# The forward recurrence pinned to one written order, with column-tiled matmuls in a few long blocks and the fold of the chain in fp32

## The chip, the cores and the metric

The kernel runs on one core of a Trainium2 chip. Its time is the device time of one execution, from the first to the last instruction with a little around it; the median of several executions is quoted. The engines have names as in the profile: PE is TensorE (PEld its weight loads), DVE is VectorE, ACT is ScalarE, POOL is GpSimd, and SP is SyncE, which here only issues DMA transfers.

## The reference

Forward and backward pass of one transformer block with conditioning. The part around the change is the attention, which is a recurrence: 2048 rows are cut into 64 segments of 32 rows, and each segment attends over 8 memory rows and its own 32 rows, where the memory is the first 8 output rows of the segment before.

```python
for s in range(n_seg):                                  # 64 segments
    h = concatenate([mem, x[:, s*32:(s+1)*32]], axis=1) # 8 + 32 rows, 512 wide
    q, k, v = h @ Wq, h @ Wk, h @ Wv                    # 32 heads of 128
    p = softmax(where(mask, q @ k.T * scale, -1e9))
    o = (p @ v) @ Wo                                    # 40 rows, 512 wide
    mem = o[:, :8]                                      # to the next segment
    outs.append(o[:, 8:])
```

Around it stand a layer norm with scale and shift, a gated MLP with its own layer norm, and the gradients of all inputs and weights.

## The kernel before

The program has five stages: the forward recurrence (`phase2`, with the first layer norm, `phase1_setup`, worked in between), the MLP forward and backward (`phase3`), weight gradients of the MLP, the backward recurrence (`phase4`) and the weight gradients of the attention (`phase5`). The change touches `phase2` and helpers that it calls.

`phase2` loops over segments `s`; `s4 = s % 4` is the place in a group of four segments, that is of 128 rows. In one segment:

- `hT` holds 8 memory columns and 24 columns of the layer-normed input, transposed. `proj(x, hf, eng)` multiplies it by one half of the heads of Wq, Wk or Wv: 16 column-tiled matmuls (stationary operand 32 columns wide, four of them side by side in the array, each to its own 32 partitions of a PSUM bank `pass_ps`), and `eng` copies the bank to rows `RA..`. `turn(x, hf, eng)` transposes these rows with four full-array matmuls (`turn_ps`) and `to_heads` spreads them over `QT`, `KT` or `VT` with three copies on `eng`.
- The last 8 rows of the four segments of a group don't depend on the chain. Their projections (`proj_b`, from `hb`, 16 column-tiled matmuls each) and transposes (`turn_b`) are put as pieces in named slots of the segments (`b_pieces`, `fill`); `to_heads("pool", ...)` copies them in.
- `st_exp(pi)` makes scores of four (the last time three) groups of heads and ACT writes their exponentials to `ET`. `vst(pi)` transposes V, `den(pi)` sums the denominators and DVE inverts them (`rden`), `pv(pi)` multiplies by V and DVE scales into `Ost`, `ott(pi)` transposes to `OT`.
- `outproj` multiplies `OT` by `Wo`: 32 column-tiled matmuls that add up in four column groups of one bank, `at_ps`. The four groups must be added: `fold_split` makes a bf16 high part (ACT, `at_hi`) and a bf16 rest (DVE, `at_lo`) of each half of the bank, and `fold_sum` adds the groups with eight small matmuls against `foldsel` (`at_ft`). ACT copies 8 columns of `at_ft` into the next segment's `hT`. That closes the chain. `TailRows` does the same for the last 8 rows of each group (`ao_tps`), in pieces called by `tail.chunk()`.
- A transposing DMA turns `ET` into `Pst`; POOL multiplies it by `rden` (`norm`), and SP stores it (`PS`). Other stores go through SP too: rows of K and Q (`KST`, `QST`), `VT`, `Ost` (`OSR`), `OT`.
- `p1(j, k)` is step `k` of the layer norm of 128 rows two groups ahead: 0 loads the rows, 1 takes their statistics (`BN_STATS` on DVE), 2 scales them, 3 shifts them, stores them and transposes them.

A scheduler turns the program into one instruction order for each engine: it takes the instructions by its own estimate of when they could start, so what stands in an engine's queue need not be the order of the code. Each engine then works its queue strictly in order and waits at an instruction whose semaphores are not there yet. SP works its DMA issues in order in the same way.

Of the kernel before, what the change touches and what calls it, by code (L numbers as in the profile page):

```python
# [40 lines left out]
class K:  # L41
# [73 lines left out]
    def phase0(self):  # L115
# [10 lines left out]
        nc.vector.tensor_tensor(self.foldsel[:], fs2[:, 0, :], fs2[:, 1, :], op=ALU.add)  # L126
        self.later = []
# [117 lines left out]

    def fold_split(self, pool, ps, name):
# [3 lines left out]
        for h in range(2):  # L250
            sl = slice(256 * h, 256 * h + 256)
            hi = pool.tile([128, 256], BF16, name=name + "_hi", tag=f"hi{h}")
            nc.scalar.activation(hi[:], ps[:, sl], AF.Copy)  # L253
            parts.append(hi)
        for h in range(2):
            lo = pool.tile([128, 256], BF16, name=name + "_lo", tag=f"lo{h}")
# [52 lines left out]
    def phase1_setup(self, ctx, psum_tile_fn):  # L309
# [11 lines left out]
        def p1_tile(j):  # L321
# [23 lines left out]
            def turn():  # L345
                h1 = p1w.tile([128, D], BF16, name="h1", bufs=1)
                nc.vector.tensor_tensor(h1[:], st["xh"][:], sa_bc[:], op=ALU.add)
                nc.gpsimd.dma_start(self.H1ROWS[j * 128:(j + 1) * 128, :], h1[:])
                tp = psum_tile_fn()
                for c in range(DC):  # L350
                    nc.tensor.transpose(tp[:, c, :], h1[:, c * 128:(c + 1) * 128], self.ident[:])
# [6 lines left out]
            return load, stats, scale, turn  # L358
# [11 lines left out]
    def phase2(self):  # L370
# [6 lines left out]
        with ExitStack() as ctx:  # L377
# [45 lines left out]
            def p1(j, k=None):  # L423
                if j < NT:
                    if j not in p1s:
                        p1s[j] = p1_tile(j)
                    for i in (range(1, 4) if k is None else [k]):
# [6 lines left out]
            with tc.tile_pool(name="p0", bufs=1) as p0:  # L434
# [10 lines left out]
                p1(0, 3)  # L445
                for f in zeros:
# [72 lines left out]
            def b_pieces(t):  # L519
# [17 lines left out]
                return {(0, "end1"): [P("v", 0)], (1, "end1"): [P("v", 1)], (1, "end2"): [P("k", 0)], (2, "mid"): [T_("v")],  # L537
                        (2, "end1"): [P("k", 1)], (2, "end2"): [P("q", 0)], (3, "end1"): [P("q", 1)], (3, "end2"): [T_("k")],
                        (4, "start"): [T_("q")]}

            first = b_pieces(0)
            q_first = [first.pop(k)[0] for k in ((2, "end2"), (3, "end1"), (4, "start"))]
# [11 lines left out]
            tail = TailRows(self, sb2, psp, psb, 1, "ao", self.AOB)  # L554
            for s in range(NS):
                s4 = s % nseg_t
                if s4 == 0:
                    p1(s // nseg_t + P1_AHEAD, 0)
                    carried = slots.pop((4, "start"), [])
                    slots = {}  # L560
                    if s + nseg_t < NS:
                        slots.update(b_pieces(s // nseg_t + 1))
# [5 lines left out]
                bt = btails[s // nseg_t]  # L568
# [6 lines left out]
                def turn(x, hf, eng):  # L575
                    if hf == 0:
                        to_heads("pool", XT[x], bt[x][:], 0, 8, 32, 8, 8 * s4)
# [1128 lines left out]
```

## Time and profile before

| | |
|---|---|
| median of three runs | 3587.64 us (3587.45 to 3591.0) |
| the profiled execution | 3587.19 us, of which the span of the instructions is 3585.4 us |
| PE | 3262.0 us busy, 39586 matmuls |
| DVE / ACT / POOL | 1655.4 / 1189.8 / 1077.9 us busy |
| mean granted TensorE clock | 0.966 of full |
| the recurrence, 60 to 1285 us | PE busy 1097 of 1225 us, granted clock 0.96, DMA engines busy 0.64 |

A busy PE is no PE at its peak: matmuls overlap, so that busy times of a group say less than the distance from the start of one to the start of the next. The time of the recurrence is best read as the distance from one segment's copy into `hT` to the next one's.

### The profile page before, as it was taken

What the parts mean: (1) busy time and instruction counts of PE and PEld (TensorE: products, weight loads), DVE (VectorE), ACT (ScalarE), POOL (GpSimd) and SP (SyncE); (2) the same over time, 40 slices, a digit from 0 to 9 for tenths busy, and PEclk for the clock granted to TensorE, in tenths of its full rate; (3) what the DMA queues carried; (4) which work ended last, traced back from release to release, by engine and by line L of the source; (5) the groups of instructions that cost most, each with busy time, mean ns of one, the idle gap of its engine ahead of it and who ended that gap; (6) DMA issues with size and microseconds to landing.
All of it is one profiled execution on the core that took longest, in us unless ns stands there. A gap on an engine that the chain in (4) does not pass through costs nothing.

```text
span 3585.4 us, 96873 instructions
## 1 busy us (share of the span) xinstructions
PE 3262.0 (91%) x39586; PEld 1763.8 (49%) x39662; DVE 1655.4 (46%) x4224; ACT 1189.8 (33%) x2714; POOL 1077.9 (30%) x2260
## 2 busy tenths in 40 slices
PE   5898899888899968996998999999999996999999
PEld 2555455455555534442554555555555553445454
DVE  4444444445454447674234555555555552322212
ACT  2444444444454433332122333333333331100011
POOL 2333333333333325553112222222222221322321
PEclk8999999999999989998999999999999998999999
DMA  8566656566676668886789999999999998887776
GB/s 272 125 135 138 139 131 134 128 134 129 132 137 142 146 177 212 202 199 188 230 230 213 236 240 240 230 242 237 236 241 239 239 228 218 232 217 200 205 199 171
DMA packets 880890, 692.19 MB, mean 193 GB/s; under 512 B 591014, under 2 KB 756150, under 8 KB 880316
## 3 DMA queue, kind: packets, MB, share of 16 engines
q1 hardware_dynamic: 786204, 501.90, 63.0%
q0 software_dynamic: 39488, 135.58, 11.9%
q10 hardware_dynamic: 54752, 48.50, 5.1%
q8 instruction: 311, 5.10, 0.6%
q14 instruction: 135, 1.11, 0.1%
HBM read 292.29 MB, written 275.02 MB: 158 GB/s over the span
## 4 chain that ended last, share of the span: by engine, by line
PE 41%; issue 6%; DMA 3%; POOL 2%; ACT 0%; DVE 0%; SPq 0%; POOLq 0%; ACTq 0%; DVEq 0%
PE dh_ps L211 10%; PE gps L1514 7%; PE pass_ps L222 5%; PE g_ps L1257 4%; PE dh_tps L211 3%; PE gps5o L1524 3%; PE gps L994 3%; PE tps L1189 2%; DMA rows<-OSR 1%; PE dp_ps L1243 1%; PE turn_ps L229 1%; PE dp_ps L1247 1%; POOL out_dram L1518 1%; DMA Kst<-KST 1%; PE dh_ft L266 1%
## 5 line engine op out<-in xcount | busy, mean ns | idle before, releaser
L1514 PE MATMUL gps<-rows,hrows 128*128 128x512 bf16 (+2 forms) x2124 | 415.1, 355 | 1.9
L1514 PEld LDWEIGHTS <-hrows 128*128 128x128 bf16 x2160 | 211.3, 98 | 204.0
L711 POOL TENSOR_TENSOR Pst<-Pst,rden 120x1408 bf16<-120x1408 bf16 x64 | 162.1, 2532 | 429.8 <-DMA Pst<-ET 295.8
L222 PEld LDWEIGHTS <-hT 128*32 128x32 bf16 x6144 | 166.8, 99 | 141.9 <-issue 24.0
L63 DVE CAST ot<-gps 128x512 bf16<-128x512 f32 (+3 forms) x77 | 48.8, 634 | 372.0 <-PE gps L1514 201.9
L257 DVE TENSOR_TENSOR dh_lo<-dh_ps,dh_hi 128x256 bf16<-128x256 f32 x128 | 48.3, 419 | 330.5 <-ACT dh_hi L253 330.5
L211 PE MATMUL at_ps<-Wo,OT 128*32 128x512 bf16 x2048 | 174.6, 384 | 22.3 <-ACT OT L61 22.3
L61 ACT ACTIVATE dVT<-g_ps 128x512 bf16<-128x512 f32 (+1 forms) x192 | 107.8, 561 | 249.9 <-issue 107.9
L61 ACT ACTIVATE ot<-gps 128x512 bf16<-128x512 f32 (+3 forms) x77 | 42.4, 550 | 397.1 <-PE gps L1514 251.9
L1518 POOL DMA_DIRECT2D out_dram<-ot x108 | 81.2, 752 | 284.9 <-DVE ot L63 142.2
L222 PE MATMUL pass_ps<-Wv,hT 128*32 128x512 bf16 x2048 | 144.3, 425 | 5.2 <-ACT hT L700 5.2
L61 ACT ACTIVATE OT<-tps 128x512 bf16<-128x512 bf16 (+1 forms) x192 | 107.7, 561 | 121.8 <-PE tps L608 92.9
L211 PE MATMUL dh_ps<-WvT,dVT 128*32 128x512 bf16 x2048 | 145.8, 383 | 0.0
L61 ACT ACTIVATE dQT<-g_ps 128x512 bf16<-128x512 f32 (+1 forms) x192 | 107.8, 561 | 109.9 <-PE g_ps L1257 107.1
L1524 PE MATMUL gps5o<-dyrows,rows 128*128 128x512 bf16 x588 | 134.9, 388 | 3.9 <-DMA rows<-OSR 3.3
L222 PE MATMUL pass_ps<-Wk,hT 128*32 128x512 bf16 x2048 | 137.4, 384 | 0.0
L211 PE MATMUL dh_ps<-WkT,dKT 128*32 128x512 bf16 x2048 | 134.0, 382 | 0.0
L222 PE MATMUL pass_ps<-Wq,hT 128*32 128x512 bf16 x2048 | 134.0, 382 | 0.0
L622 DVE TENSOR_TENSOR Ost<-or_ps,rden 120x512 bf16<-120x512 f32 (+1 forms) x192 | 124.0, 646 | 15.8
L257 DVE TENSOR_TENSOR at_lo<-at_ps,at_hi 128x256 bf16<-128x256 f32 x128 | 48.2, 418 | 173.9 <-PE pass_ps L222 151.1
L222 PE MATMUL pass_ps<-WoT,dyT 128*32 128x512 bf16 x2048 | 123.5, 383 | 4.9 <-ACT dyT L1330 4.9
L63 DVE CAST dKT<-g_ps 128x512 bf16<-128x512 f32 (+1 forms) x192 | 122.3, 637 | 10.9 <-PE g_ps L1257 9.5
(379 smaller groups left out, 7275.6 us busy)
## 6 DMA issues: line engine op xcount, KB each, us to landing
OSR<-Ost SPq DMA_DIRECT2D x64, 352.0 KB
OT<-OT SPq DMA_DIRECT2D x64, 352.0 KB
PS<-Pst SPq DMA_DIRECT2D x64, 352.0 KB
OT_l<-OT SPq DMA_DIRECT2D x64, 352.0 KB
Pst_l<-PS SPq DMA_DIRECT2D x64, 352.0 KB
DVR<-rows_x POOLq DMA_DIRECT2D x64, 352.0 KB, 4.7
DKR<-rows_x POOLq DMA_DIRECT2D x64, 352.0 KB, 5.7
DQR<-rows_x POOLq DMA_DIRECT2D x64, 352.0 KB, 4.2
```

Of the source, the lines that this page charges most:

```text
L61: return nc.scalar.activation(out, in_, AF.Copy)
L63: return nc.vector.tensor_copy(out, in_)
L211: self.nc.tensor.matmul(ps[32 * j:32 * j + 32, :], lhsT=lhsT, rhs=w, start=(n < 4), stop=(n >= total - 4), tile_position=(0, 32 * j))
L222: self.nc.tensor.matmul(ps[32 * j:32 * j + 32, :], lhsT=lhs(c), rhs=rhs, start=(c == 0), stop=(c == DC - 1), tile_position=(0, 32 * j))
L257: nc.vector.tensor_tensor(lo[:], ps[:, 256 * h:256 * h + 256], parts[h][:], op=ALU.subtract)
L622: nc.vector.tensor_tensor(part3(Ost, pi)[0:120, 0:n, :], or_ps[0:120, 0:n, :], rden[:, pi * PG:pi * PG + n].unsqueeze(2).to_broadcast([120 ...
L711: nc.gpsimd.tensor_tensor(Pst[0:120, :, :], Pst[0:120, :, :], rden[:, :].unsqueeze(2).to_broadcast([120, G, 128]), op=ALU.mult)
L994: nc.tensor.matmul(ps[:], lhsT=h2r[:, j, c * 128:(c + 1) * 128], rhs=xr[:, j, :], start=(j == 0), stop=(j == NT - 1))
L1257: nc.tensor.matmul(ps[:, j, :], lhsT=lh[:, g * GW:(g + 1) * GW], rhs=rh[:, g * GW:(g + 1) * GW], start=True, stop=True)
L1514: nc.tensor.matmul(ps[:, 0:ng * E], lhsT=hrows[:, tp_, c * 128:(c + 1) * 128], rhs=rows[:, tp_, 0:ng * E], start=(tp_ == 0), stop=(tp_ == ...
L1518: nc.gpsimd.dma_start(outw[c * 128:(c + 1) * 128, h0:h0 + 3 * (ng - 1) + 1:3, :], ot[:, 0:ng * E].rearrange("p (h e) -> p h e", e=E))
L1524: nc.tensor.matmul(ps[:], lhsT=rows[:, tp_, gg * E:(gg + 1) * E], rhs=dyrows[:, tp_, :], start=(tp_ == 0), stop=(tp_ == NTP - 1))
```

## The change

- Order: `pin` ties every instruction that the loop over segments issues to the one before it on its engine, in the order of the code. The scheduler can no longer move any of them past another, on PE, DVE, ACT, POOL or SP.
- The code of a segment is written in a new order: six `proj` in a row, then six `turn`, one piece of 16 column-tiled matmuls (slot `f1`) behind the first scores, a second one (slot `f2`) behind `outproj`, which now is one block of 32. The tail's chunks are two of 16, both in the fourth segment.
- The fold: ACT copies the left half and DVE the right half of `at_ps` as fp32 to one tile `at_part`, and four fp32 matmuls against an fp32 `foldsel32` replace eight bf16 ones.
- Engines: `turn` of K and Q goes to DVE and of V to ACT; the last copy to `OT` goes to DVE.
- Layer norm: step 0 is at the start of a group as it was, the statistics now stand in the second segment behind the projections of V; shift and transposes are two steps.
- `Pst`'s transposing DMA is issued right behind the last scores, `Ost` and `OT` are stored before the fold instead of at the end, `norm` moves to the start of the next segment, and the copies of the group's last rows (`tails_in`) are made one segment ahead.

```diff
+    def pin(self, i0):
+        last = {}
+        for ins in self.traced()[i0:]:
+            e = ins.engine
+            if e in last:
+                self.tc.add_manual_dep(ins, last[e].name, ..., reason="program order")
+            last[e] = ins
+    def fold_parts(self, pool, ps, name):
+        t = pool.tile([128, 512], F32, name=name + "_part", tag="part", bufs=1)
+        self.evac("act", t[:, 0:256], ps[:, 0:256])
+        self.evac("dve", t[:, 256:512], ps[:, 256:512])
+        return t
+    def fold32(self, psp, part, name, tag):
+        ft = psp.tile([128, self.cfg.DC, 32], F32, name=name + "_ft", tag=tag)
+        for c in range(self.cfg.DC):
+            self.nc.tensor.matmul(ft[:, c, :], lhsT=part[:, c * 128:(c + 1) * 128], rhs=self.foldsel32[:], start=True, stop=True)
+        return ft
...
+                return {(0, "f1"): [P("v", 0)], (0, "f2"): [P("v", 1)], (1, "f1"): [P("k", 0)], (1, "f2"): [P("k", 1)], (1, "w4"): [T_("v")],
+                        (2, "f1"): [P("q", 0)], (2, "f2"): [P("q", 1)], (2, "w4"): [T_("k")], (3, "turn"): [T_("q")]}
...
+                if norms:
+                    norms.pop()()
                 proj("v", 0, "act")
                 proj("v", 1, "dve")
-                if s4 == 0:
-                    for f in carried:
-                        f()
+                if 1 <= s4 <= 3:
+                    p1(s // nseg_t + P1_AHEAD, s4)
                 proj("k", 0, "act")
-                turn("v", 0, "dve")
+                proj("k", 1, "dve")
+                proj("q", 0, "dve")
+                proj("q", 1, "act")
...
-                proj("q", 0, "dve")
+                turn("k", 0, "dve")
+                turn("q", 0, "dve")
+                turn("v", 0, "act")
                 turn("v", 1, "act")
+                turn("k", 1, "dve")
+                turn("q", 1, "dve")
                 nc.sync.dma_start(self.VT[s], VT[:, :])
...
                 st_exp(0)
                 vst(0)
+                fill(s4, "f1")
+                if s4 == 3:
+                    tail.chunk()
+                st_exp(1)
                 vst(1)
-                self.pop_later()
                 vst(2)
                 den(0)
                 pv(0)
-                st_exp(1)
                 st_exp(2)
-                fill(s4, "mid")
+                fill(s4, "turn")
...
+                    tails_in("kqv", s + 1)
+                Pst = sb2.tile([128, G, 128], BF16, name="Pst", bufs=1)
+                nc.sync.dma_start(Pst[:], ET[:, :], transpose=True)
...
                 ott(2)
-                if norms:
-                    norms.pop()()
-                outproj(12, 24)
-                outproj(24, H)
-                parts = self.fold_split(sb2, at_ps[0], "at")
+                nc.sync.dma_start(self.OSR[s], gl3(Ost))
+                outproj(0, H)
+                part = self.fold_parts(sb2, at_ps[0], "at")
                 tail.collect(s4, [OT])
-                fill(s4, "end1")
+                nc.sync.dma_start(self.OT[s], gl3(OT))
+                fill(s4, "f2")
...
-                ft = self.fold_sum(psp, parts, "at", "p")
+                ft = self.fold32(psp, part, "at", "p")
...
+            self.pin(i0)
```

Three places of the resulting order matter for what follows. First DVE, in the queue between the last scaling into `Ost` and the fold. Before, at the end of a group's fourth segment, the statistics of a layer-norm tile (`x_1` is the tile of loaded rows) stand ahead of the bf16 rest of the fold:

```order
L622 TENSOR_TENSOR Ost_157<-or_ps,rden 120x384 [waits DVE_49]
L331 BN_STATS st_13901<-x_1_13274 128x6 [waits DMAHW0_49]
L333 BN_AGGR mv_13903<-st_13901 128x2 [waits DVE_49]
L335 TENSOR_SCALAR ve_13905<-mv_13903 128x1 [waits DVE_49]
L257 TENSOR_TENSOR at_lo<-at_ps,at_hi 128x256 [waits PE_49,Activation_49]
```

Now, from the end of a group's first segment into the second, the same engine has:

```order
L653 TENSOR_TENSOR Ost_159<-or_ps,rden 120x384 [waits DVE_49,PE_49]
L63 COPY OT_160<-tps 128x384 [waits DMAHW5_49,PE_49,Pool_49]
L63 COPY at_part<-at_ps 128x256 [waits Activation_49]
L63 CAST RBv_166<-pass_ps 128x512 [waits PE_49]
L302 CAST at_tb<-at_ft 128x128 [waits Activation_49]
L63 CAST RA0v_161<-pass_ps 128x512 [waits PE_49]
L359 BN_STATS st_11884<-x_1_11467 128x6 [waits DMAHW6_49]
L361 BN_AGGR mv_11886<-st_11884 128x2 [waits DVE_49]
L363 TENSOR_SCALAR ve_11888<-mv_11886 128x1 [waits DVE_49]
L63 CAST RA1k_164<-pass_ps 128x512 [waits DMAHW7_49,PE_49]
```

The statistics moved from the end of the fourth segment to the second segment, behind the fold; the right half of the fold waits for ACT, whose half of the same bank comes first.

On PE at the fold in a group's second segment, before:

```order
L222 LDWEIGHTS hb
L222 MATMUL pass_ps<-Wv,hb 32x512
L266 LDWEIGHTS at_hi
L266 MATMUL at_ft<-foldsel,at_hi 128x32
L222 LDWEIGHTS hb
L222 MATMUL pass_ps<-Wk,hb 32x512
```

and now:

```order
L224 LDWEIGHTS hb
L224 MATMUL pass_ps<-Wk,hb 32x512
L271 MATMUL at_ft<-foldsel_94,at_part 128x32 x4
L231 LDWEIGHTS RBv_166
L231 MATMUL turn_ps<-ident,RBv_166 128x128
```

Full-array matmuls of the fold no longer stand between column-tiled ones; `x4` are the four fp32 matmuls, which have no weight-load instruction of their own in this list.

On SP, from the transposing DMA of a group's fourth segment to that of the next segment, before:

```order
L683 DMA_TRANSPOSE Pst<-ET_155 128x11x128
L327 DMA x_1_19602<-in_A_x_dram 128x512
L707 DMA OSR<-Ost_157 128x1408
L708 DMA OT<-OT_158 128x1408
L713 DMA PS<-Pst 128x1408
L510 DMA QST<-RBq_166 4x8x1024 x3
L513 DMA QST<-RBq_166 4x8x384 x2
L652 DMA VT<-vT_154 128x1328
L504 DMA KST<-RA0k_160 3x32x1024
L506 DMA KST<-RA0k_160 32x3x384
L504 DMA QST<-RA0q_161 3x32x1024
L506 DMA QST<-RA0q_161 32x3x384
```

and now:

```order
L710 DMA_TRANSPOSE Pst<-ET_157 128x11x128
L725 DMA OSR<-Ost_159 128x1408
L729 DMA OT<-OT_160 128x1408
L355 DMA x_1_13013<-in_A_x_dram 128x512
L744 DMA PS<-Pst 128x1408
L535 DMA KST<-RA0k_162 3x32x1024
L537 DMA KST<-RA0k_162 32x3x384
L535 DMA QST<-RA0q_163 3x32x1024
L537 DMA QST<-RA0q_163 32x3x384
L691 DMA VT<-vT_156 128x1328
L710 DMA_TRANSPOSE Pst<-ET_157 128x11x128
```

The store of `Pst` now has only stores of rows and of `VT` between itself and the next transposing DMA; the stores of the group's last rows (`RBq`) no longer stand there.

More of the change, by code (lines that the diff above doesn't have):

```diff
@@ L356, in turn @@
                 return hx, hb
-            return load, stats, scale, turn
+            return load, stats, scale, shift, turn
         return p1_tile
@@ L426, in p1 @@
                         p1s[j] = p1_tile(j)
-                    for i in (range(1, 4) if k is None else [k]):
+                    for i in (range(1, 5) if k is None else [k]):
                         r = p1s[j][i]()
@@ L445, in phase2 @@
                 p1(0, 3)
+                p1(0, 4)
                 for f in zeros:
@@ L558, in phase2 @@
                     p1(s // nseg_t + P1_AHEAD, 0)
[L559 to L562, printed above, removed]
+                    slots = b_pieces(s // nseg_t + 1) if s + nseg_t < NS else {}
                 hT = get_ht(s)
```

59 lines of the change are left out of this document (27 added, 32 removed).

## The prediction

> **What bounds the kernel now.** I read the page first, then the busy time by stretch, then the list of waits, then the timeline of one disturbed and of one clean segment.
>
> ```profile
> span 3585.4 us, 96873 instructions
> 60.00:1285.00 1225.00, 1097.07 (x16875) 627.15 (x16875) 594.41 (x1801) 565.23 (x1471) 412.29 (x1067) 0.96 0.64 135
> 603.50:610.40 6.90, 4.29 (x45) 1.91 (x45) 3.38 (x10) 1.28 (x3) 4.17 (x7) 0.51 0.52 191
> ```
>
> The recurrence takes about 1225 us of the span, and PE is busy for 90% of it (the columns behind the length are PE, PEld, DVE, ACT, POOL, then granted clock, DMA share and GB/s). Only this stage changes, so the question is the length of a segment. One copy into `hT` closes each segment; the distance between these copies is that length. First all from the fourth copy on, then one group of four that has a stall, then one that has none:
>
> ```profile
> L700 ACT ACTIVATE hT<-at_ft x59: 192/197/198, 149.0 to 1269.7; 128x32 bf16<-128x32 f32 x59
> L700 ACT ACTIVATE hT<-at_ft x5: 192/197/197, 529.3 to 606.9; 128x32 bf16<-128x32 f32 x5
> L700 ACT ACTIVATE hT<-at_ft x5: 197/197/198, 1145.0 to 1215.0; 128x32 bf16<-128x32 f32 x5
> ```
>
> That is (1269.7 - 149.0) / 58 = 19.32 us for a segment on average, 77.6 us for the group with the stall and 70.0 us (17.50 each) for the clean one. The stall is in the waits:
>
> ```profile
> DVE st L331 <- DMA x<-in_A_x_dram: 102.9, 13, 10.4
> PE at_ft L266 <- DVE at_lo L257: 83.8, 16, 8.6
> ```
>
> ```profile
> 595.45 4.51 SPq L683 DMA_TRANSPOSE Pst<-ET  x1
> 600.05 1.25 SPq L327 DMA_DIRECT2D x<-in_A_x_dram  x1
> 604.77 0.69 DVE L331 BATCH_NORM_STATS2 st<-x 128x6 f32<-128x512 bf16 x1 [7.85 <-DMA x<-in_A_x_dram]
> 605.38 0.74 DVE L257 TENSOR_TENSOR at_lo<-at_ps,at_hi 128x256 bf16<-128x256 f32 x2
> 605.84 0.21 PE L266 MATMUL at_ft<-foldsel,at_lo 128*128 128x32 bf16 x1 [5.99 <-DVE at_lo L257]
> ```
>
> SP issues the load of the layer-norm rows at 600.05, behind a transposing DMA that held it for 4.51 us. DVE has come to the statistics of these rows and stands there for 7.85 us; the fold's `at_lo` is behind them in DVE's queue, and PE waits 5.99 us for it. Then PE works at half clock (0.51 from 603.5 to 610.4). This happens thirteen times, once in a group.
>
> **The removed stall.** In the new order the load is issued at the start of a group and the statistics stand in its second segment, a whole segment (over 16 us) later; between issue and landing lay under 5 us above. SP has nothing to wait for ahead of the load but the stores of `Ost` and `OT`. So DVE does not wait there, and PE does not lose clock. I cost the statistics themselves at nothing: 0.69 us on DVE during the projections, where DVE has only bank copies. If that were all, a segment would be 17.50.
>
> **The new segment, laid out on PE.** The order is fixed now, so I build it from durations of a clean segment. t = 0 is the first matmul on `hT`.
>
> ```profile
> 1235.01 1.91 PE L222 MATMUL pass_ps<-Wv,hT 128*32 128x512 bf16 x32 [0.29 <-ACT hT L700]
> 1236.75 1.04 PE L222 MATMUL pass_ps<-Wk,hT 128*32 128x512 bf16 x16
> 1237.72 0.40 PE L229 MATMUL turn_ps<-ident,RA0v 128*128 128x128 bf16 x4
> 1238.05 1.05 PE L222 MATMUL pass_ps<-Wq,hT 128*32 128x512 bf16 x16
> 1239.03 0.40 PE L229 MATMUL turn_ps<-ident,RA0v 128*128 128x128 bf16 x4
> 1241.86 0.23 PE L585 MATMUL st_ps<-qT,kT 128*128 128x120 bf16 x1
> 1242.29 0.39 PE L608 MATMUL tps<-ident,vT 128*128 128x128 bf16 x4
> 1242.52 0.39 PE L229 MATMUL turn_ps<-ident,RA1k 128*128 128x128 bf16 x4
> 1243.41 0.24 PE L599 MATMUL dc_ps<-ones,ET 128*128 128x1 bf16 x4
> 1243.77 0.21 PE L585 MATMUL st_ps<-qT,kT 128*128 128x120 bf16 x1
> 1248.21 1.32 PE L211 MATMUL at_ps<-Wo,OT 128*32 128x512 bf16 x20
> 1250.02 0.19 PE L266 MATMUL at_ft<-foldsel,at_hi 128*128 128x32 bf16 x1 [0.49 <-ACT at_hi L253]
> 1251.15 0.18 PE L266 MATMUL at_ft<-foldsel,at_lo 128*128 128x32 bf16 x1
> 1251.61 0.61 PE L222 MATMUL pass_ps<-Wv,hT 128*32 128x512 bf16 x8 [0.29 <-ACT hT L700]
> ```
>
> ```profile
> 1239.51 0.72 ACT L61 ACTIVATE vT<-turn_ps 128x384 bf16<-128x384 bf16 x3 [1.07 <-PE turn_ps L229]
> 1239.76 0.54 DVE L63 COPY kT<-turn_ps 128x384 bf16<-128x384 bf16 x3
> 1243.52 0.41 DVE L613 COPY Vst<-tps 128x512 bf16<-128x512 bf16 x1
> 1246.66 0.56 DVE L622 TENSOR_TENSOR Ost<-or_ps,rden 120x384 bf16<-120x384 f32 x1
> 1251.36 0.20 ACT L700 ACTIVATE hT<-at_ft 128x32 bf16<-128x32 f32 x1 [1.12 <-PE at_ft L266]
> ```
>
> Pace: 32 column-tiled matmuls from 1235.01 to 1236.75 are 0.054 us each; four transposes from 1242.29 to 1242.52 are 0.056 each; eight score matmuls from 1241.86 to 1242.29 are 0.054 each. A change between column-tiled and full-array costs 0.11 us each way: the sixteen at 1238.05 need 0.98 until the next transpose instead of 0.87, the four at 1237.72 need 0.33 until the next column-tiled instead of 0.22. A segment has 14 to 18 such changes before (the fold and `at_ps` are cut up) and six now, which is 0.9 to 1.3 us less. What else is in the way:
>
> - 96 projections, 5.22, and a change: the transposes start at 5.33. The 24 of them and one of a store end at 6.73.
> - DVE spreads K and Q, 0.54 a half, and ACT V, 0.72 a half, each about 0.45 behind its transposes (1239.03 to 1239.51). The first scores need K and Q's first halves (5.33 + 0.43 + 2 x 0.54 = 6.84); the transposes of V need ACT's second half, which begins at 5.33 + 0.45 + 0.45 + 0.72 = 6.95 and gives its first copy about 7.3. Scores and four transposes end about 7.57.
> - Slot `f1`: a change, 16 matmuls, a change: 8.66. Before, this piece stood in the shadow of the fold; now it is paid in full, 1.09 us.
> - Eight scores, seven transposes, four denominators and four products (0.36, 1243.41 to 1243.77), six scores: about 10.1. In between, the second `Vst` copy can start on DVE at 9.08 + 0.43 = 9.51.
> - From here DVE sets the pace: `Vst`, `rden` and three scalings. In the clean segment they run from the second `Vst` copy to the end of the last `Ost`, 1243.52 to 1247.22, 3.70 us. The list is the same, so `Ost` ends at 13.2; PE waits some 2 us in three places. The last transposes and a change: `outproj` starts at 13.54.
> - 32 matmuls: 20 took 1.32, so 1.32 + 12 x 0.054 = 1.97, ending at 15.51. Slot `f2` is issued behind them and is free of waits until 16.26.
>
> **The fold.**
>
> ```profile
> L253 ACT ACTIVATE at_hi<-at_ps 128x256 bf16<-128x256 f32 x128 | 42.1, 381 | 53.4 <-PE at_ps L211 53.4
> L257 DVE TENSOR_TENSOR at_lo<-at_ps,at_hi 128x256 bf16<-128x256 f32 x128 | 48.2, 418 | 173.9 <-PE pass_ps L222 151.1 <-ACT at_hi L253 22.8
> 1250.77 0.10 PEld L266 LDWEIGHTS <-at_hi 128*128 128x128 bf16 x1
> ```
>
> ACT's half is there at 15.95 (0.06 and 0.381 behind the last matmul, as the 0.49 before 1250.02 shows). DVE's half waits for ACT's by the new order, so the two engines don't work at once: 0.05 and 0.42 more, 16.42. Before, the same stretch took 1248.21 + 1.32 = 1249.53 to 1251.61, 2.08 us, with four copies in a row.
>
> The trace has no fp32 matmul. Below, the four go at the pace of the eight of now (0.025 each): the last two wait for DVE's half and their sum is there at 16.47 + 0.05 + 0.18 = 16.70. Above, each fp32 operand counts as two bf16 parts and each product of parts as a pass with a full weight load of 0.10 that nothing hides: 16 passes, 1.6 us from 16.26. I take the row of a full load with a stream of 128 columns that overlaps, 0.056 as in the transposes, since a weight load of 128 columns is what both share: 16 x 0.056 = 0.90 from 16.26, with 0.18 for the last, 17.34. From there to the next projection it is 0.28 (1251.33 to 1251.61).
>
> So a segment is 17.6 (ends: 17.0 and 18.3). In the second and third segment eight transposes stand behind the fold (0.45 and a change), 0.1 more than the copy they hide: 17.65 on average (17.03 and 18.36). In the fourth, eight or twelve more transposes lie in DVE's waits.
>
> The Trainium skill, FP8 and Floating Point Precision (TensorE Precision Notes), says that true FP32 takes four passes through the array, and TensorE: Matmul & The Clock Gate (Weight-path perf modes) that fp32 inputs get no fast weight load; its figure of P/1.2 ns makes 107 ns for 128 columns. By these pages the fold would be an estimated 16 x 0.107 + 0.18 = 1.9 us and the time about 3529 us. No run here shows it yet.
>
> **The sum.** Against the profiled execution (3587.2 us, 0.4 below the median): 60 segments from the fifth on, and one stall of 7.6 us (77.6 - 70.0) in the first group, whose start-up I leave as it is. 3587.2 - 60 x (19.32 - 17.65) - 7.6 = 3479 us; the ends of the fold give 3442 and 3522. So the written order and the fold are worth about nothing against a clean segment (17.50); nearly all is the removed stall.
>
> **The rivals.**
>
> - The transposing DMA becomes the bound. SP's store of `Pst` must wait for POOL's product, and the next transposing DMA is behind that store.
>
> ```profile
> 1230.47 4.93 SPq L683 DMA_TRANSPOSE Pst<-ET  x1
> 1239.78 2.53 POOL L711 TENSOR_TENSOR Pst<-Pst,rden 120x1408 bf16<-120x1408 bf16 x1 [7.89 <-DMA Pst<-ET]
> 1242.34 0.32 SPq L713 DMA_DIRECT2D PS<-Pst  x1
> 1246.57 4.56 SPq L683 DMA_TRANSPOSE Pst<-ET  x1
> ```
>
> This loop takes 16.1 us without the stores of a group's last rows, which leave it now. With 17.65 it has 1.5 us to spare, and POOL, whose `norm` now stands ahead of the next copies of last rows, has the same. If landing takes 2 us longer because those stores now run beside it, the loop is 18.1 and the time 3587.2 - 60 x 1.22 - 7.6 = 3506.
> - The fold at its upper price, a full unhidden load for each pass: 3522. The kernel's own trace has no row against it.
> - Slower than before: each pass loads, streams and drains before the next begins, 0.10 + 0.18 as a single fold matmul, 16 x 0.28 = 4.5 us. A segment is then 16.26 + 4.5 + 0.28 = 21.0 and the time 3682. It decides from 2.9 us for the fold (0.73 per fp32 matmul) on. Against it: the bf16 ones start 0.025 apart, so passes don't wait for a drain.
> - No change: the pinned queues wait as much as the stall took, 1.8 us a segment more than I found. For it speaks that the scheduler no longer fills any gap; against it that each wait above is already counted.
>
> **How the numbers follow.** My layout 0.67, the upper fold 0.14, the DMA loop 0.10, slower 0.06, no change 0.03. I predict 3478. The layout's own range is 3442 to 3522; for 8 in 10 I go to 3425 (0.3 us a segment where copies on DVE overlap more than I let them) and to 3545 (upper fold and 0.4 us of waits). A measurement tells about 0.2%, 7 us, from no change; faster by more than that has 0.91.
>
> **What would show it.** Right: no wait of the statistics for the load and no half clock in the recurrence; copies to `hT` about 17.6 us apart and alike in all four segments; PE waiting before the last transposes of `Ost`; fp32 matmuls about 0.22 apart. Wrong: copies over 18.5 apart, the wait of the scores' exponentials or of SP for `Pst`, or fp32 matmuls over 0.4 apart.

## The result and the profile after

The changed kernel takes 3456.4 us (median, 3448.9 to 3466.8) against 3589.3 us before: a ratio of 0.963, 95% interval 0.961 to 0.966. In a second comparison it was 0.967 (0.965 to 0.969). The forecast was 3478 us with a range from 3425 to 3545. The profiled execution took 3466.8 us. From it the page's first line, the busy time of the recurrence and of the seven microseconds that had the stall before, and the row of all copies into `hT`:

```profile
span 3465.0 us, 96579 instructions
```

```profile
60.00:1148.00 1088.00, 1011.72 (x16852) 651.64 (x16844) 643.67 (x1992) 473.60 (x1156) 408.43 (x1072) 1.00 0.70 152
603.00:610.00 7.00, 6.94 (x131) 5.06 (x121) 4.96 (x20) 3.95 (x11) 1.30 (x5) 1.00 0.55 123
```

```profile
L735 ACT ACTIVATE hT<-at_ft x63: 197/197/197, 59.3 to 1131.6; 128x32 bf16<-128x32 f32 x63
```

PE is busy for 93% of the recurrence instead of 90%, the granted clock is 1.00 instead of 0.96, and the copies are (1131.6 - 59.3) / 62 = 17.30 us apart. Before, the last of them stood at 1269.7: the recurrence gives 138 us. A clean segment of the changed kernel in the timeline, PE first, then DVE, ACT and PE's weight loads:

```profile
1015.50 1.91 PE L224 MATMUL pass_ps<-Wv,hT 128*32 128x512 bf16 x32 [0.38 <-ACT hT L735]
...
1020.79 0.40 PE L231 MATMUL turn_ps<-ident,RA0k 128*128 128x128 bf16 x4
...
1023.08 1.05 PE L224 MATMUL pass_ps<-Wv,hb 128*32 128x512 bf16 x16
...
1025.75 0.24 PE L630 MATMUL dc_ps<-ones,ET 128*128 128x1 bf16 x4
...
1026.54 0.40 PE L639 MATMUL tps<-ident,Ost 128*128 128x128 bf16 x4 [0.30 <-DVE Ost L653]
...
1028.30 0.34 PE L639 MATMUL tps<-ident,Ost 128*128 128x128 bf16 x3 [0.48 <-DVE Ost L653]
1028.57 1.91 PE L213 MATMUL at_ps<-Wo,OT 128*32 128x512 bf16 x32
1030.31 1.04 PE L224 MATMUL pass_ps<-Wv,hb 128*32 128x512 bf16 x16
1031.28 1.08 PE L271 MATMUL at_ft<-foldsel,at_part 128*128 128x32 f32 x8
1032.73 1.05 PE L224 MATMUL pass_ps<-Wv,hT 128*32 128x512 bf16 x16 [0.38 <-ACT hT L735]
```

```profile
1024.92 0.69 DVE L644 COPY Vst<-tps 128x512 bf16<-128x512 bf16 x2 [1.23 <-PE tps L639]
...
1027.68 0.56 DVE L653 TENSOR_TENSOR Ost<-or_ps,rden 120x384 bf16<-120x384 f32 x1
...
1030.95 0.42 DVE L63 COPY at_part<-at_ps 128x256 f32<-128x256 f32 x1 [1.86 <-ACT at_part L61]
```

```profile
1030.53 0.38 ACT L61 ACTIVATE at_part<-at_ps 128x256 f32<-128x256 f32 x1 [2.02 <-PE at_ps L213]
```

```profile
1031.27 0.97 PEld L271 LDWEIGHTS at_ft<-foldsel,at_part 128*128 128x128 f32 x8 [0.42 <-ACT at_part L61]
```

The waits of the statistics for the load and of PE for `at_lo` are gone; of PE's waits in the recurrence the longest in sum is the one for DVE's `Ost`:

```profile
PE tps L639 <- DVE Ost L653: 50.4, 152, 0.8
PE pass_ps L224 <- ACT hT L735: 9.5, 25, 0.4
```

Not all of the 138 us arrive at the end: the backward recurrence, whose own program text is untouched, became longer. The copies into `dyT` close its segments; first before, then after:

```profile
L1330 ACT ACTIVATE dyT<-dh_ft x63: 197/197/198, 1920.2 to 2959.8; 128x32 bf16<-128x32 f32 x63
```

```profile
L1362 ACT ACTIVATE dyT<-dh_ft x63: 192/197/197, 1779.9 to 2842.5; 128x32 bf16<-128x32 f32 x63
```

That is 1039.6 against 1062.6 us, 23 us given back. The stages between the two recurrences and behind them are 3 us shorter each, so that the two profiled executions differ by 120 us (3587.2 and 3466.8); the median of the changed kernel lies 10 us below its profiled execution.

### The profile page after: what moved, and what is told of

Its sections match the earlier page's. It is cut to its first block, busy times and chain, and to the rows that moved or that the text cites. A ratio compares the mean times of both kernels' runs of the same rounds, so it can differ in the third digit from the quotient of the medians.

```text
span 3465.0 us, 96579 instructions
## 1 busy us (share of the span) xinstructions
PE 3190.6 (92%) x39586; PEld 1793.8 (52%) x39662; DVE 1701.8 (49%) x4417; ACT 1098.3 (32%) x2394; POOL 1074.7 (31%) x2260
## 3 DMA queue, kind: packets, MB, share of 16 engines
q14 instruction: 133, 1.09, 0.1%
## 4 chain that ended last, share of the span: by engine, by line
PE 39%; issue 8%; DMA 6%; POOL 2%; ACT 1%; DVE 0%; SPq 0%; POOLq 0%; ACTq 0%; DVEq 0%
PE dh_ps L213 10%; PE gps L1546 7%; PE pass_ps L224 5%; PE g_ps L1289 4%; PE dh_tps L213 3%; PE gps5o L1556 3%; DMA Kst<-KST 3%; PE tps L1221 2%; DMA rows<-OSR 1%; PE turn_ps L231 1%; PE dp_ps L1275 1%; PE dp_ps L1279 1%; POOL out_dram L1550 1%; PE dh_ft L294 1%; PE gps L1026 1%
## 5 line engine op out<-in xcount | busy, mean ns | idle before, releaser
L65 POOL COPY vT<-b_colsv 128x24 bf16<-128x24 bf16 (+2 forms) x256 | 50.4, 241 | 322.0 <-DMA VT<-vT 313.3
L224 PE MATMUL pass_ps<-WoT,dyT 128*32 128x512 bf16 x2048 | 131.7, 402 | 9.3 <-ACT dyT L1362 9.3
L1296 POOL DMA_DIRECT2D DQR<-rows_x x64 | 34.5, 539 | 332.9 <-DMA rows_x<-dQT 101.6
L224 PE MATMUL pass_ps<-Wv,hT 128*32 128x512 bf16 x2048 | 122.2, 380 | 12.4 <-ACT hT L735 9.7
L1026 PE MATMUL gps<-xr,h2r 128*128 128x448 bf16 x512 | 105.3, 357 | 21.4 <-DMA xr<-DGROWS 21.4
L639 PE MATMUL tps<-ident,Ost 128*128 128x128 bf16 x704 | 72.6, 222 | 55.2 <-DVE Ost L653 51.2
L213 PE MATMUL at_ps<-Wo,OT 128*32 128x512 bf16 x2048 | 122.3, 380 | 0.0
```

Source lines behind the costliest of these rows:

```text
L213: self.nc.tensor.matmul(ps[32 * j:32 * j + 32, :], lhsT=lhsT, rhs=w, start=(n < 4), stop=(n >= total - 4), tile_position=(0, 32 * j))
L224: self.nc.tensor.matmul(ps[32 * j:32 * j + 32, :], lhsT=lhs(c), rhs=rhs, start=(c == 0), stop=(c == DC - 1), tile_position=(0, 32 * j))
L639: nc.tensor.transpose(ps[:, j, :], src[:, g * w:g * w + GW], self.ident[:, :])
L1026: nc.tensor.matmul(ps[:], lhsT=h2r[:, j, c * 128:(c + 1) * 128], rhs=xr[:, j, :], start=(j == 0), stop=(j == NT - 1))
```

## The experiments

For each kernel, the distance from one segment's first matmul on `hT` to the next one's in the forward recurrence, averaged by place in the group, the last copy into `hT` (one profiled execution each), and the ratio to the kernel before with its interval:

| kernel | first | second | third | fourth | last `hT` | ratio |
|---|---|---|---|---|---|---|
| before | 20.07 | 17.86 | 17.57 | 22.75 | 1269.7 | 1 |
| late_stats | 19.43 | 21.34 | 17.32 | 17.47 | 1232.0 | 0.993 (0.991 to 0.995) |
| late_chain | 20.41 | 17.50 | 17.47 | 17.51 | 1189.0 | 0.979 (0.976 to 0.981) |
| late_norm | 18.36 | 17.58 | 17.81 | 17.13 | 1157.4 | 0.967 (0.965 to 0.969) |
| changed (after_again) | 17.34 | 17.15 | 17.17 | 17.63 | 1129.9 | 0.967 (0.965 to 0.969) |
| no_pin | 19.10 | 17.57 | 17.11 | 29.56 | 1344.4 | 1.026 (1.024 to 1.028) |
| bf16_fold | 17.28 | 17.06 | 17.15 | 17.92 | 1132.8 | 0.966 (0.963 to 0.968) |
| two_bufs | 17.34 | 17.14 | 17.24 | 17.66 | 1132.2 | 0.965 (0.963 to 0.967) |
| moved_f1 | 16.52 | 16.23 | 17.79 | 16.68 | 1098.7 | 0.953 (0.950 to 0.955) |
| short_loop | 19.21 | 16.50 | 17.23 | 20.13 | 1189.1 | 0.979 (0.977 to 0.981) |
| late_rows | 18.88 | 16.45 | 16.30 | 21.22 | 1184.2 | 0.978 (0.976 to 0.981) |

The edits below are shortened: `...` stands for lines left out, and words in angle brackets for an expression that finds the instruction named.

### Is the stall the gain? late_stats, late_chain, late_norm, no_pin

**late_stats** holds one instruction of the kernel before:

```diff
+                if s4 == 1:                               # behind proj("v", 1, "dve")
+                    p1(s // nseg_t + P1_AHEAD, 1)
+                    self.tc.add_manual_dep(<its first instruction>, <DVE's last one>, ...)
...
-                if s4:
+                if s4 > 1:
                     p1(s // nseg_t + P1_AHEAD, s4)
```

> The kernel before with one edit: the statistics of the layer-norm rows may not stand in DVE's queue before the second projection copy of a group's second segment. The scheduler still orders everything else, the fold stays in bf16, pieces stay where they were. Theory 'the stall is nearly all': 13 stalls of 7.6 us go, 99 us, and at most 117 if every segment comes to 17.5 us: 3472 to 3490 us, ratio 0.967 to 0.973. Rival 'the written order and the new fold are what pays': less than 40 us are gained, 3549 us or more, ratio above 0.989.

It took 3554 us, a ratio of 0.993. By the number that is the rival's range, but neither theory had the reason: the fourth segments lost their stall (22.75 to 17.47), and the second ones got one (17.86 to 21.34). DVE's and PE's waits say why:

```profile
DVE xh L342 <- POOL rstd L337: 46.8, 14, 5.3
```

```profile
PE turn_ps L229 <- DVE RA1q L63: 40.9, 12, 5.0
```

The scheduler puts the scaling right behind the statistics. It needs `rstd` from POOL, where this small step stands behind the product on `Pst`, and the copy to `RA1q` that PE needs is behind the scaling in DVE's queue.

**late_chain** holds statistics, scaling and shift, each in its own segment:

```diff
                 proj("v", 1, "dve")
+                mark = <the last instruction>
...
                 if s4:
                     p1(s // nseg_t + P1_AHEAD, s4)
+                    self.tc.add_manual_dep(<its first instruction>, mark.name, ...)
```

> The kernel before, with all three steps of the layer-norm rows held back on DVE: statistics, scaling and shift each not before the second projection copy of its own segment (second, third, fourth of a group). In late_stats only the first was held, and the next one took its place: DVE stood 46.8 us, 14 times, at the scaling for POOL's rstd, and the long segments moved from the last of a group (22.7 us on average) to the second (21.3). Theory 'DVE's queue is the stall, whichever step stands in it': with all three held, no segment has it; the long ones come to about 17, 15 x 5.8 = 88 us less, 3500 us, ratio 0.975. Rival 'another cross-engine wait takes its place again': above 3540, ratio above 0.987. Rival 'with the stall gone it is worth what the whole change was': 3465, ratio 0.967.

The first theory holds in the main: 0.979 where it had 0.975, and no place but the first of a group is above 17.51. The recurrence is 81 us shorter. What is left is in the first segments, where PE waits for POOL:

```profile
PE st_ps L585 <- POOL qT L65: 25.7, 9, 6.2
```

**late_norm** adds one more hold, at `norms.pop()()`:

```diff
+                    for x in "kq":
+                        self.tc.add_manual_dep(<POOL's product>, <its copy of last rows into x>.name, ...)
```

> late_chain with one more hold: POOL's product on Pst may not stand ahead of the copies of last rows into kT and qT of its segment. In late_chain the scheduler puts it ahead of them once in a group, and in these first segments PE waits 25.7 us (9 times, up to 6.2) for POOL's qT; first segments are 20.4 us on average, the undisturbed ones 18.4. Theory 'these first segments are what the written order still gains beside DVE's stall': 16 x 2 = 32 us less than late_chain, 3479 us, ratio 0.970, and the recurrence (1205 us in late_chain, 1148 in the changed kernel) at 1173. Rival 'the product only comes late elsewhere': SP's store of Pst and the next transposing DMA move back, PE waits for the exponentials instead, and the ratio stays within 0.977 to 0.981.

The wait left the list, the first segments are at 18.36, and the ratio is 0.967, the same as that of the whole change. So four holds on the old code, three on DVE and one on POOL, are worth what the change is worth. Added in this order, the holds on DVE's queue give 81 of the 138 us of the recurrence (late_chain), POOL's product standing ahead of the last rows 32, and all else that was rewritten 26. What the hold on POOL gives without the others was not tried, and neither was the pin on the old code. late_norm's backward recurrence has 1043.1 us from first to last copy into `dyT`, 20 less than the changed kernel's, which is why it draws level.

**no_pin** is the changed code without its last line, `self.pin(i0)`.

> The changed kernel without the pin at the end of the forward recurrence: the same code, left to the scheduler. It puts the statistics right behind the load again, in the first segment of a group. Theory 'the stall is nearly all': it comes back, 13 times about 7.6 us or 99 us, so 3555 us, ratio 0.99. Rival 'the new places in the code and the new fold suffice, the pin changes nothing': 3456 us, ratio 0.963. Rival 'the scheduler's filling is worth something': below 0.963.

It is slower than before, 3674 us. DVE's wait came back as expected, and a larger one beside it, which had not been expected:

```profile
DVE st L359 <- DMA x<-in_A_x_dram: 95.8, 12, 9.7
```

```profile
PE ao_tps L213 <- POOL ao_tail L1613: 154.8, 15, 11.8
```

The tail's chunks are now two blocks of 16 instead of four of 8; left free, the scheduler puts them ahead in PE's queue, before POOL has collected the rows. Without the pin the rewritten code is slower than the kernel before.

### The backward recurrence: after_again, two_bufs, before_one_buf

The change has one more edit, in a function that the backward recurrence shares: `fold_split` allocates its four parts with one buffer instead of the pool's two.

```diff
-            hi = pool.tile([128, 256], BF16, name=name + "_hi", tag=f"hi{h}")
+            hi = pool.tile([128, 256], BF16, name=name + "_hi", tag=f"hi{h}", bufs=1)
```

> The changed kernel once more, as the yardstick for its variants. Both theories: ratio to before near 0.963. What it tells apart is the fourth phase (the backward recurrence, from the first pass_ps<-WoT to the last dh_ft), which took 1100.0 us against 1076.6 before although its program text differs only in fold_split. Theory 'one buffer': the phase is again 1095 to 1105 us. Rival 'a passing disturbance of that one execution': it is 1073 to 1080 us here.

It was no passing disturbance: 1099.5 us again from the first `pass_ps<-WoT` to the last `dh_ft`.

The tail's fold (`dh_b`) and the chain's (`dh`) use the same parts. Before, at the end of a group's third segment (ACT, then PE):

```profile
2573.44 0.66 ACT L253 ACTIVATE dh_hi<-dh_ps 128x256 bf16<-128x256 f32 x2 [2.38 <-PE dh_ps L211]
2573.98 0.67 ACT L253 ACTIVATE dh_b_hi<-dh_tps 128x256 bf16<-128x256 f32 x2
...
2574.61 0.19 PE L266 MATMUL dh_ft<-foldsel,dh_lo 128*128 128x32 bf16 x1 [0.54 <-DVE dh_lo L257]
...
2575.22 0.20 ACT L1330 ACTIVATE dyT<-dh_ft 128x32 bf16<-128x32 f32 x1 [0.57 <-PE dh_ft L266]
...
2575.47 1.91 PE L222 MATMUL pass_ps<-WoT,dyT 128*32 128x512 bf16 x32 [0.29 <-ACT dyT L1330]
```

After, at the same place, and the granted clock (the first of the last three numbers) behind it:

```profile
2445.24 0.19 PE L294 MATMUL dh_ft<-foldsel,dh_lo 128*128 128x32 bf16 x1 [0.54 <-DVE dh_lo L285]
...
2445.49 0.76 ACT L281 ACTIVATE dh_b_hi<-dh_tps 128x256 bf16<-128x256 f32 x2 [0.77 <-PE dh_ft L294]
2446.15 0.19 ACT L1362 ACTIVATE dyT<-dh_ft 128x32 bf16<-128x32 f32 x1
...
2446.39 3.29 PE L224 MATMUL pass_ps<-WoT,dyT 128*32 128x512 bf16 x32 [0.59 <-ACT dyT L1362]
```

```profile
2446.40:2449.40 3.00, 3.00 (x32) 1.07 (x32) 0.84 (x3) 0.60 (x1) 0.00 (x0) 0.56 1.27 113
```

With one buffer `dh_b_hi` waits until the chain's fold has read `dh_hi`, and then stands ahead of the chain's own copy `dyT`. PE waits 0.30 us longer, and here the next 32 matmuls run at half clock, 3.29 us instead of 1.91.

Why so short a wait can cost that much, and only in some groups, can be read from when the half clock starts. In these traces its records start on a grid of 3.41 us and last one step of it or several. The record here is 2446.76 to 2450.17. In the step before it, 2443.35 to 2446.76, PE was busy for 1.94 of 3.41 us, a share of 0.57; before the change the step that holds the same waits (2573.13 to 2576.55) had 2.25 us, 0.66, and kept full clock. In the changed kernel 8 of 15 groups have a step with 0.57 here, and 7 of these are followed by half clock and a fourth segment of about 18.5 us instead of 17.0; in the other seven the waits lie otherwise in the grid, and no step there has less than 0.59. In after_again only two groups are hit, so what the buffer costs depends on where the waits fall.

**two_bufs** gives the backward recurrence its second buffer again (`bufs=1 if self.name == "ao" else 2` for the tail's fold, 2 for `dh`).

> The changed kernel, but the backward recurrence keeps two buffers for the parts of its fold (the forward one keeps one). Theory 'one buffer': dh_b_hi no longer has to wait for the chain's fold, so it no longer stands between that fold and the copy dyT; the fourth phase goes back to about 1077 us and the time falls by about 23, to 3433 us (ratio 0.957). Rival 'passing disturbance' or 'something left over from the new third-phase timing': nothing changes, ratio 0.963 and the phase at 1100 us or wherever the yardstick has it.

**before_one_buf** puts `bufs=1` into the kernel before and changes nothing else.

> The kernel before, with one buffer instead of two for the parts of every fold, and nothing else. Theory 'one buffer costs the backward recurrence': its third segments of a group go from 16.18 to 16.48 us and some fourth ones from 17.0 to 18.5, so the fourth phase takes 1085 to 1095 us instead of 1077; the waits for Kst stay at about 3 us in all if they come from the new forward recurrence, and rise to 10 or more if they come from the buffers. The forward recurrence may move by a few us either way. Ratio 1.000 to 1.006. Rival: no change at all, phase at 1077.

The buffer is one cause, and two_bufs misses the 1077 us that were expected. In two_bufs PE's wait for `dyT` is back at 4.9 us (9.3 after), all third segments but three are at 16.2 again, and no fourth one is above 17.1. In before_one_buf that wait is 9.0, third segments are at 16.48, and the phase takes 1090.5 us, 14 more than the 1076.6 before; the whole kernel is slower by a ratio of 1.002 (1.001 to 1.004). But two_bufs' phase came down to 1093.7 only, 6 us, and the interval of its ratio overlaps that of after_again. Most of the rest goes with PE's wait for rows of K from DRAM, here in two_bufs and in the kernel before:

```profile
PE g_ps L1289 <- DMA Kst<-KST: 15.9, 11, 3.8
```

```profile
PE g_ps L1257 <- DMA Kst<-KST: 3.1, 3, 1.4
```

and the half clock behind some of these waits. The wait is 10 to 16 us in the changed kernel (both executions), two_bufs, moved_f1 and late_rows, and 3 to 7 us in the others; but short_loop, which has the pin and the fp32 fold too, is among these with 6.2, and in two_bufs SP, POOL, ACT and DVE issue this stage in the same order as before. What makes these loads land late is open.

### The fold: bf16_fold

```diff
-                part = self.fold_parts(sb2, at_ps[0], "at")
+                parts = self.fold_split(sb2, at_ps[0], "at")
...
-                ft = self.fold32(psp, part, "at", "p")
+                ft = self.fold_sum(psp, parts, "at", "p")
```

> The changed kernel with the chain's fold as it was before: four bf16 parts, two copies on ACT and two subtractions on DVE, eight bf16 matmuls. In the changed kernel's trace the fp32 fold starts when the sixteen matmuls of the second slot end (0.97 us behind the last at_ps) and needs 0.80 to its last pass and 0.28 for that, 1.08: it ends at 2.05. Theory 'the fp32 fold costs PE more than it saves the copies': in bf16 the last part is there at 0.06 + 0.38 + 2 x 0.42 = 1.28, and four matmuls 0.10 and 0.18 behind it, 1.6: 0.4 us a segment less, 63 x 0.4 = 25 us, 3439 us, ratio 0.960 where the yardstick has 0.967. Rival 'fewer copies pay': 0.5 us a segment more because ACT and DVE serve the same bank in turn, 3495 us, ratio 0.975.

Neither: 0.966 against 0.967. The copies are slower than expected and the matmuls faster:

```profile
1031.10 0.66 ACT L281 ACTIVATE at_hi<-at_ps 128x256 bf16<-128x256 f32 x2 [2.08 <-PE at_ps L213]
...
1031.79 0.76 DVE L285 TENSOR_TENSOR at_lo<-at_ps,at_hi 128x256 bf16<-128x256 f32 x2 [2.13 <-ACT at_hi L281]
...
1031.84 0.19 PE L294 MATMUL at_ft<-foldsel,at_hi 128*128 128x32 bf16 x1
1032.27 0.19 PE L294 MATMUL at_ft<-foldsel,at_lo 128*128 128x32 bf16 x1 [0.24 <-DVE at_lo L285]
```

DVE's first half starts behind ACT's second, not behind its first, so four copies run in a row and end at 1032.55, 0.7 us behind the end of slot `f2` (1031.84). That eats what the eight short matmuls save over the fp32 ones. Between the two folds no difference shows.

### Slack in the changed kernel: moved_f1, short_loop, late_rows

**moved_f1** is two_bufs with slot `f1` at another place:

```diff
                 vst(0)
-                fill(s4, "f1")
-                if s4 == 3:
-                    tail.chunk()
                 st_exp(1)
...
                 pv(2)
+                fill(s4, "f1")
+                if s4 == 3:
+                    tail.chunk()
                 ott(1)
+                while held:          # the copy of f1's bank
+                    held.pop()()
```

> The changed kernel with two buffers in the backward recurrence (as two_bufs) and the pieces of slot f1 moved from between the first Vst copy and the second scores to behind the last product, ahead of the last two groups of transposes of Ost; the copy of the piece's bank is issued behind ACT's OT copy. In the changed kernel's trace f1 takes 1.09 us that nothing hides, while PE waits 1.8 us in four places behind DVE's chain of Vst, rden and Ost. Theory 'DVE's chain sets the pace and PE has room in it': the chain starts 1.09 earlier and a segment falls by about 0.9 to 16.3; 60 x 0.9 = 54 us less than two_bufs, 3404 us, ratio 0.950. Rival 'the loop of SP's transposing DMA, POOL's product and the store of Pst, 16.1 us, becomes the bound': segments of 16.5 to 17 with the first exponential waiting, 20 to 40 us less, ratio 0.954 to 0.960. Rival 'PE is the bound': no gain, ratio 0.965.

The first theory holds for three places of a group: 3418 us, 0.953 (0.950 to 0.955), against 0.965 for two_bufs and 0.967 for after_again. PE's rows where `f1` now stands: the last two groups of transposes and `at_ps` follow without a wait:

```profile
678.78 1.05 PE L224 MATMUL pass_ps<-Wk,hb 128*32 128x512 bf16 x16
679.76 0.56 PE L643 MATMUL tps<-ident,Ost 128*128 128x128 bf16 x7
680.25 1.91 PE L213 MATMUL at_ps<-Wo,OT 128*32 128x512 bf16 x32
```

The third segments stayed at 17.8, and the reason is in neither theory. PE's longest wait of this recurrence in sum is there, for a copy on DVE; behind it one of the third segments, DVE and POOL:

```profile
PE turn_ps L232 <- DVE RA0q L63: 19.9, 12, 2.4
```

```profile
618.26 3.51 DVE L371 TENSOR_SCALAR xh<-x,mv,rstd 128x512 f32<-128x512 bf16 x1
618.94 2.54 POOL L748 TENSOR_TENSOR Pst<-Pst,rden 120x1408 bf16<-120x1408 bf16 x1
```

The copy to `RA0q` stands behind the scaling of the layer norm. In five of the fourteen groups that have it in this loop the scaling takes 0.54 to 0.77 us; in the other nine it meets POOL's product on `Pst`, takes 1.78 to 3.51 us and ends 0.28 to 0.30 us behind the product each time. In late_rows below no scaling meets the product, all fourteen take 0.54 us, and third segments are at 16.3. So the scaling stood while POOL worked on its product (and on two small copies right ahead of it), and the late first exponential follows from that.

**short_loop** was to shorten the loop of transposing DMA, product and store: V's last rows behind POOL's product, and SP's stores of `RBk` and `RBq` behind the store of `Pst`. **late_rows** is the second half alone.

```diff
                 if norms:
                     norms.pop()()
+                    tails_in("v", s)          # short_loop only
+                while rows_b:                 # both: stores of RBk, RBq
+                    rows_b.pop(0)()
```

> moved_f1 with POOL's copy of V's last rows behind the product on Pst instead of ahead of it (there it waits up to 8.6 us for SP's store of VT, 361 us in all, and the product behind it), and with SP's stores of RBk and RBq behind the store of Pst. In moved_f1 three segments of a group take 16.2 to 16.7 us but the third takes 17.8, its first exponential at 9 to 10.5 us instead of 7.4. Theory 'the loop of transposing DMA, product and store bounds that segment': the product starts 1 to 2 us earlier, the stores free 4 us of SP's queue, and third segments fall to 16.3; 16 x 1.5 = 24 us less than moved_f1, 3394 us, ratio 0.946. Rival 'the DMA engines themselves are at their limit there': same time, ratio 0.9527. Rival 'V's last rows come too late for the transposes of V': 1 us a segment more, ratio 0.970.

> moved_f1 with the other half of short_loop alone: SP's stores of RBk and RBq stand behind the store of Pst instead of ahead of it; POOL's copy of V's last rows stays where it is. In short_loop that copy came too late (PE waited 78.8 us for it, 35 times), which hid what the stores do. Theory 'in the third segment SP's 4.3 us of stores ahead of the store of Pst hold the loop': third segments fall from 17.8 towards 16.4, up to 20 us, ratio 0.947 to 0.950. Rival 'the stores only move the delay to the stores behind them, VT and the next transposing DMA are as late': same as moved_f1, ratio 0.9527.

Both are misses, 0.979 (0.977 to 0.981) and 0.978 (0.976 to 0.981). Third segments did fall, to 17.2 and 16.3, but fourth ones rose to 20.1 and 21.2, and first ones to 19.2 and 18.9. First POOL's wait in moved_f1, then in late_rows, then PE's in short_loop:

```profile
POOL vT L65 <- DMA VT<-vT: 361.3, 62, 8.6
```

```profile
POOL vT L65 <- DMA VT<-vT: 695.7, 63, 14.2
```

```profile
PE tps L645 <- POOL vT L65: 78.8, 35, 4.7
```

The loop that binds in these two has `VT` in it: SP's store of `VT` lands, POOL copies V's last rows, then comes its product, then SP's store of `Pst`, then the next store of `VT`. Ahead of the store of `Pst` SP had time for the stores of `RBk`, since it waited for the product anyway; behind it they are a part of the loop. This account is read from the queues and the waits; no run takes the store of `VT` out of the loop. V's last rows alone behind the product were not tried.

## Why the prediction was right, point by point

- **The stall.** Right in place (fourth segments fall from 22.75 to 17.5, 5.2 us on average over all groups), but the reason given was too narrow. Not the load alone holds DVE's queue: late_stats shows that the next step of the same tile takes its place at another engine's result. What removed it is the pin, which keeps all three steps apart; that "a whole segment" between load and statistics suffices would have been wrong without it.
- **"Nearly all is the removed stall."** Too much: 81 of 138 us. A second wait, POOL's product ahead of the last rows, held 32 us; it was in the average of 19.32 that the sum started from, so the sum had it without naming it. The written order and the fold give 26 where the prediction had about nothing.
- **The segment**, 17.65 forecast, 17.23 measured in the clean one above. Up to the chain on DVE the layout holds within 0.1 (transposes 5.29 against 5.33, slot `f1` to 8.56 against 8.66). The mis-sized term is the chain from the second `Vst` copy to the end of `Ost`: 3.70 forecast, 1024.92 to 1028.24 measured, 3.32. The duration was taken whole from a segment of before in which it contained a wait behind the second exponential (PE, then DVE, which loses about 0.25 us by it) and a copy of the tail's fold, about 0.15 us, that does not stand there in the segment above:

```profile
1245.07 0.25 PE L599 MATMUL dc_ps<-ones,ET 128*128 128x1 bf16 x4 [0.41 <-ACT ET L589]
```

```profile
1243.85 0.21 DVE L280 COPY ao_b_rb<-ao_b_tp 128x128 bf16<-128x128 bf16 x1
1245.36 0.18 DVE L601 RECIPROCAL rden<-dc_ps 120x4 f32<-120x4 f32 x1 [0.16 <-PE dc_ps L599]
```

  In the new order the second exponential is done by then (no wait at 1025.75).
- **Slot `f1` paid in full**, 1.09 forecast, 0.8 to 1.0 measured: moved_f1 takes it out of the way, and against two_bufs the first, second and fourth segments fall by 0.82, 0.91 and 0.98.
- **The fold**, 1.08 forecast from 16 passes of 0.056 and 0.18; 1.08 measured, but made otherwise: the trace has two records for each fp32 matmul, 0.11 apart, and 0.28 for the last. The Trainium skill (FP8 and Floating Point Precision, TensorE Precision Notes) says four passes through the array: four of 0.056 would make the 0.22 of a matmul, but the trace has two records and does not show the passes, so the hit on 1.08 is partly luck. The 1.9 us that the prediction estimated from the Trainium skill (TensorE: Matmul & The Clock Gate, LDWEIGHTS) did not come: each load takes 0.19 us in the trace and overlaps the pass before.
- **The halves on two engines** run one behind the other, as forecast (ACT at 1030.53, DVE at 1030.95), and cost nothing, since slot `f2` ends at 1031.28 when DVE's is all but done.
- **The DMA loop** as a rival did not come in the changed kernel. What its four segments over 18 us (18.1 to 19.4) share is something else, which the prediction did not see: in each a layer-norm step on DVE meets POOL's product on `Pst` and takes 2.0 to 3.2 us instead of 0.5 to 0.7, as in moved_f1. A loop with `VT` in it binds in short_loop and late_rows.
- **What failed** is the tacit step that only the forward recurrence changes. The backward one took 23 us more. A shared helper with one buffer less is one cause (14 us when it alone is put into the kernel before, 6 us back when it is undone in the changed one), later loads of K are another. The sum had 108 us from the forward recurrence and got 138: 15 more from the segment (17.33 on average over the 58 from the fifth copy on), and 15 more from the first group (22 us instead of the 7.6 of one stall). These 30 us and the 23 us nearly cancel, so by luck the time came out closer than its terms.

## What to carry to other kernels

An engine's in-order queue is blocked by whatever a scheduler places early for a result that another engine or a transfer owes; to remove such a wait hold the whole chain of that tile's steps, since the next step takes the place of the one removed. Before one rewrites an order, a few holds on the old one are worth a try: here four gave the same time. A step that is long in some segments and short in others has to be read beside what the other engines do at that moment. Take a chain's length from rows without waits of their own, and look at who else calls a helper whose buffers change.

## What the runs showed of the hardware

- An fp32 matmul with 128 x 128 weights and 32 columns costs 0.22 us in a row of four and shows as two records, each with a weight load of 0.19 us; the bf16 one costs 0.025.
- Half clock needed no long pause: 0.56 for 3 us behind waits of 0.54 and 0.59 us that lie 1.2 us apart, where 0.54 and 0.29 at the same place before left it at full. In the traces of this case half clock starts on a grid of 3.41 us. Counted over both recurrences of all thirteen traces, each of the 97 grid steps at full clock in which PE was busy for less than 0.40 was followed by half clock, and none of the 7824 with 0.70 or more; in between both happen.
- The Trainium skill, TensorE: Matmul & The Clock Gate (What's actually happening), names an idle window of about 3.4 us ahead of half rate. The length agrees with the grid here; but PE was busy for 1.94 of the 3.41 us before 2446.76, so the step need not be idle, and the measurement decides.
- A step on DVE can stand while POOL works: in moved_f1 the scaling of 128x512 took 0.54 us alone and up to 3.51 us beside POOL's product of 2.54 us, and each of the nine long ones ended 0.28 to 0.30 us behind the product.
